# A gated linear-attention block feeding a two-layer feed-forward: units 0 to 13 interleaved step by step, and an earlier issue of the weights

## The chip, the core and the metric

The kernel runs on one core of a Trainium2 chip. The metric is the device time of one execution in microseconds (us), taken as the median of several runs. Besides these times there is one execution recorded by the hardware profiler; all starts and durations below come from it.

The core's engines work from queues of their own, each in order: PE (TensorE) multiplies matrices and writes its sums to PSUM, and its weight loads are shown as PEld; DVE (VectorE), ACT (ScalarE) and POOL (GpSimd) work on whole tiles; SP (SyncE) here only issues DMA transfers. An instruction starts when the ones before it in its queue are through and the results that it needs are there.

## The reference

```
f = 1/(1+exp(-f_logit))                        # batch 4, heads 8, 768 steps, 48 wide
for t:  state = f[t] * state + outer(k[t], v[t])      # 48 x 48 for each head
        y[t]  = q[t] @ state
x   = y, the heads side by side                # 3072 tokens x 384
h   = x @ w_in                                 # 384 -> 2048
out = max(0.01*h, h) @ w_out                   # 2048 -> 384
```

All inputs and the output are float32 in device memory. The kernel multiplies in bfloat16 and sums in float32.

## The kernel before

**Units.** The 768 steps are cut into 6 chunks of 128. One chunk of one batch is a unit, with all 8 heads; there are 24 units, chunk by chunk (units 0 to 3 are the first chunk of the four batches). Units 2x and 2x+1 are pair x. A unit goes through these steps, each a function; the letters are those that the changed kernel uses.

- **L**, `load` (L73-80): four DMAs from SP's queue, f, k, q, v in this order, 192 KB each. The tiles have 9 buffers, so nine units can be held.
- **A**, `gate_act` (L108-113): on ACT, exp and ln(1+.) turn f_logit into minus the logarithm of the gate (`lf`).
- **G**, `gate` (L115-140): on PE, a product with a triangle of ones sums `lf` along the chunk into the PSUM tile `cs`, with four narrow products for the sum at the chunk's end. ACT makes `em_t`, `a_t` and `a_end` out of it by exp. Then k is scaled by em_t (L134, on DVE for units under 13, else on POOL) and q by a_t (L135, on POOL, for unit 3 on DVE), into the two halves of the tile `kq`. For units from `TURN_DMA` = 13 on, a DMA from SP's queue then transposes `kq` into `kqT` (L138).
- **V**, `cast_v` (L142-150): two casts of v on POOL.
- **T**, `turn` (L152-162), for units under 13: PE transposes `kq`, four matmuls for the k half and four for the q half, into the PSUM tile `tp`; DVE copies each half to `kqT` after its four.
- **S**, `score` and `mask` (L164-178): eight matmuls k by q into two PSUM tiles `pw`, then two DVE multiplications by the triangle give `wm`.
- **X**, `mix` (L186-208): `wm` by v, and, from the second chunk on, the state by q, summed on PE into `py`; a DVE cast stores it as half of the pair's `xT`.
- **P**, `state` (L210-225): on PE, k by v into `pt`; two DVE additions, one POOL multiplication and two POOL casts make the state for the same batch's next chunk.
- **U** and **u**, `up2` (L233) and `up1` (L243): the first layer. `up2` gives two of the 16 hidden blocks for both units of a pair (6 matmuls of 256 columns), `up1` four blocks for one unit (12 matmuls of 128 columns). ACT applies the leaky rectifier, reading the PSUM tile `pm`, which has two buffers.
- **D**, `down` (L253-273): the second layer, 16 matmuls of 384 columns for a unit; a DVE copy to `osb` and an output DMA from SP's queue follow the last.

The PSUM tiles cs, tp, py and pt share one ring of two buffers (`ps_s`, tag "sm"): a new one waits until the one two before it has been read.

**Order.** `tc.manual_schedule()` is on: each engine runs its instructions in the order in which the functions are called. L276-445 are a list of calls written out by hand; the loop at L447-471 takes over at pair 5. In the list units 0 to 3 are carried through their attention first (L276-317), one after the other; the weights are fetched behind a small POOL copy that reads unit 3's q (L300), in eight cast DMAs issued by POOL (`load_w_in`, `load_w_out`); then the first layer of pairs 0 and 1 runs, and from L326 on the second layer of unit 0 and later units is mixed with the attention of units 4 to 12. A small DMA that reads the third part of w_out (L311) holds SP's queue until that part has come; the loads of units 4, 5, 6 stand behind it. In the loop, iteration i runs load(i+7), half of pair i//2's first layer, G and V of unit i+4, D of unit i-2, S of unit i+3, X and P of unit i+2.

Of the kernel before, what the change touches and what calls it, by code (L numbers as in the profile page):

```python
# [15 lines left out]
def kernel(  # L16
# [10 lines left out]
    nc = tc.nc  # L27

    B, H, S, D = q.shape
# [3 lines left out]
    P2 = H // 2  # L33
# [3 lines left out]

    units = [(c, b) for c in range(NCH) for b in range(B)]
    NU = len(units)
    TURN_DMA = 13  # L40
    NB = 4

    const = ctx.enter_context(tc.tile_pool(name="const", bufs=1))
# [16 lines left out]
    hold = const.tile([1, 4], FP32, tag="hold")  # L60
    WQ, OQ = FF // 4, NF // 4

    def load_w_in(i):
        nc.gpsimd.dma_start(out=w_in_b[:, :, i * WQ:(i + 1) * WQ],
                            in_=moe_w_in[:, i * WQ:(i + 1) * WQ].rearrange("(k p) f -> p k f", p=128))

    def load_w_out(i):
        nc.gpsimd.dma_start(out=w_out_b[:, i * OQ:(i + 1) * OQ, :],
                            in_=moe_w_out[i * OQ * 128:(i + 1) * OQ * 128, :].rearrange("(a p) n -> p a n", p=128))

    raw = {}
# [32 lines left out]
    st = {u: {} for u in range(NU)}  # L104
# [3 lines left out]
    def gate_act(u):  # L108
        if u >= NU:
            return  # L110
        e = work.tile([128, H, D], FP32, name="e_t", tag="e_t")
        nc.scalar.activation(e, raw[u]["f"], AF.Exp, scale=-1.0)  # L112
        nc.scalar.activation(lfs[u % 3][:, :, 0:D], e, AF.Ln, bias=1.0)  # L113

    def gate(u):  # L115
        c, b = units[u]
        lf = lfs[u % 3]
        cs = ps_s.tile([128, 512], FP32, name="cs", tag="sm")
        nc.tensor.matmul(cs[:, 0:H * D], ut, lf[:, :, 0:D], start=True, stop=True)  # L119
        if c < NCH - 1:  # L120
            for p in range(P2):
                nc.tensor.matmul(cs[:, H * D + p:H * D + p + 1], lf[:, 2 * p:2 * p + 2, :], ones_col,  # L122
                                 start=True, stop=True)
        a_t = work.tile([128, H, D], BF16, name="a_t", tag="a_t")
        em_t = work.tile([128, H, D], BF16, name="em_t", tag="em_t")
        nc.scalar.activation(em_t, cs[:, 0:H * D], AF.Exp, scale=1.0)  # L126
        nc.scalar.activation(a_t, cs[:, 0:H * D], AF.Exp, scale=-1.0)  # L127
        if c < NCH - 1:
            a_end = work.tile([128, P2], FP32, name="a_end", tag="a_end")
            nc.scalar.activation(a_end, cs[:, H * D:H * D + P2], AF.Exp, scale=-1.0)  # L130
            st[u]["a_end"] = a_end
        r = raw[u]
        kq = kqs[u % NB]
        (nc.vector if u < TURN_DMA else nc.gpsimd).tensor_mul(kq[:, 0, :, 0:D], r["k"], em_t)  # L134
        (nc.vector if u == 3 else nc.gpsimd).tensor_mul(kq[:, 1, :, 0:D], r["q"], a_t)  # L135
        if u >= TURN_DMA:
            kqT = work.tile([128, 2, P2, 128], BF16, name="kqT", tag="kqT")
            nc.sync.dma_start_transpose(out=kqT.rearrange("d a p t -> d (a p) t"),  # L138
                                        in_=kq.rearrange("t a h d -> t (a h d)"))
            st[u]["kqT"] = kqT  # L140

    def cast_v(u):  # L142
        r = raw.pop(u)
        v_b = work.tile([128, H, D], BF16, name="v_b", tag="v_b")
        nc.gpsimd.tensor_copy(out=v_b, in_=r["v"])  # L145
        v2 = v2s[u % NB]
        nc.gpsimd.tensor_copy(
            out=v2[:, :, 0:4:3, :],
            in_=r["v"].rearrange("t (p j) d -> t p (j d)", j=2)[:, :, 32:64].rearrange("t p (j e) -> t p j e", j=2))
        st[u]["v"], st[u]["v2"] = v_b, v2  # L150

    def turn(u):  # L152
        if u >= TURN_DMA:
            return
        kq = kqs[u % NB]
        tp = ps_s.tile([128, 2, P2, 128], BF16, name="tp", tag="sm")
        kqT = work.tile([128, 2, P2, 128], BF16, name="kqT", tag="kqT")
        for i in range(2):
            for p in range(P2):
                nc.tensor.transpose(tp[:, i, p, :], kq[:, i, 2 * p:2 * p + 2, :], ident)  # L160
            nc.vector.tensor_copy(out=kqT[:, i], in_=tp[:, i])  # L161
        st[u]["kqT"] = kqT

    def score(u):  # L164
        kqT = st[u]["kqT"]
        pws = [ps_w.tile([128, P2, 128], FP32, name="pw", tag="pw") for j in range(2)]
        for p in range(P2):
            for j in range(2):
                rows = slice(64 * j, 64 * j + D)
                nc.tensor.matmul(pws[j][:, p, :], kqT[rows, 0, p, :], kqT[rows, 1, p, :], start=True, stop=True)  # L170
        st[u]["pw"] = pws
        st[u]["wm"] = []

    def mask(u, js=(0, 1)):
        for j in js:
            wm = work.tile([128, P2, 128], BF16, name="wm", tag="wm", bufs=6)
            nc.vector.tensor_mul(wm, st[u]["pw"][j], ut[:, None, :].to_broadcast([128, P2, 128]))  # L177
            st[u]["wm"].append(wm)

    def pair(u):  # L180
        x = u // 2
# [91 lines left out]
            st.pop(u)  # L273


    gate_act(0)  # L276
    gate(0)
    cast_v(0)
    gate_act(1)
    turn(0)  # L280
    gate(1)
    score(0)
    mask(0)
    cast_v(1)
    gate_act(2)
    mix(0)
    state(0)
    turn(1)
    gate(2)
    score(1)  # L290
    mask(1)
    cast_v(2)
    gate_act(3)
    mix(1)
    state(1)
    turn(2)
    gate(3)
    score(2)
    mask(2)
    nc.gpsimd.tensor_copy(out=hold[:, 0:2], in_=raw[3]["q"][0:1, 0, 0:2])  # L300
    for i in range(4):
        load_w_in(i)
    cast_v(3)
    for i in range(4):
        load_w_out(i)
    mix(2)
    state(2)
    turn(3)
    score(3)
    mask(3)  # L310
    nc.sync.dma_start(out=hold[:, 2:4], in_=w_out_b[0:1, 2 * OQ, 0:4].bitcast(FP32))  # L311
    for u in (4, 5, 6):
        load(u)
    up2(0, 0)
    up2(0, 1)
    mix(3)
    state(3)
    up2(1, 0)
    up2(1, 1)
    for i in range(2, 8, 2):  # L320
        for x in range(2):
            up2(x, i)
            up2(x, i + 1)
    gate_act(4)

    down(0)  # L326
    down(1, 0, 8)
    gate(4)
    cast_v(4)
    gate_act(5)  # L330
    load(7)
    down(1, 8)
    down(2, 0, 8)
    turn(4)
    score(4)
    mask(4)
    down(2, 8)
    gate(5)
    cast_v(5)
    gate_act(6)  # L340
    load(8)
    down(3, 0, 8)
    mix(4)
    state(4)
    turn(5)
    down(3, 8)
    up1(4, 0)
    up1(4, 1)
    score(5)
    mask(5)  # L350
    up1(4, 2)
    gate(6)
    cast_v(6)
    load(9)
    up1(4, 3)
    mix(5)
    state(5)
    gate_act(7)
    down(4, 0, 8)
    turn(6)  # L360
    down(4, 8)
    up1(5, 0)
    score(6)
    mask(6)
    up1(5, 1)
    gate(7)
    cast_v(7)
    load(10)
    up1(5, 2)
    mix(6)  # L370
    state(6)
    up1(5, 3)
    gate_act(8)
    down(5, 0, 6)
    turn(7)
    down(5, 6, 8)
    score(7)
    mask(7)
    down(5, 8, 12)
    mix(7)  # L380
    state(7)
    load(11)
    load(12)

    def attend(u):
        gate(u)
        cast_v(u)
        gate_act(u + 1)

    up2(3, 0)  # L390
    attend(8)
    up2(3, 1)
    up2(3, 2)
    down(5, 12)
    load(13)
    turn(8)
    up2(3, 3)
    score(8)
    mask(8)
    attend(9)  # L400
    up2(3, 4)
    mix(8)
    state(8)
    load(14)
    up2(3, 5)
    up2(3, 6)
    turn(9)
    up2(3, 7)
    score(9)
    mask(9)  # L410
    down(6, 0, 6)
    attend(10)
    mix(9)
    state(9)
    load(15)

    up2(4, 0)
    up2(4, 1)
    attend(11)
    down(6, 6)  # L420
    turn(10)
    up2(4, 2)
    score(10)
    mask(10)
    up2(4, 3)
    turn(11)
    mix(10)
    state(10)
    score(11)
    mask(11)  # L430
    load(16)

    up2(4, 4)
    attend(12)
    up2(4, 5)
    down(7, 0, 8)
    attend(13)
    mix(11)
    turn(12)
    up2(4, 6)  # L440
    state(11)
    up2(4, 7)
    score(12)
    mask(12)
    down(7, 8)

    for i in range(10, NU + 2):  # L447
        x, h = divmod(i, 2)
        if i + 7 < NU:
            load(i + 7)  # L450
        if i < NU:
            up2(x, 4 * h)
            up2(x, 4 * h + 1)
        if i + 4 < NU:
            gate(i + 4)
            cast_v(i + 4)
        down(i - 2, 0, 8)
        if i < NU:
            up2(x, 4 * h + 2)
        gate_act(i + 5)  # L460
        if i + 3 < NU:
            score(i + 3)
            mask(i + 3, (0,))
        if i + 2 < NU:
            mix(i + 2)
            state(i + 2)
        if i + 3 < NU:
            mask(i + 3, (1,))
        if i < NU:
            up2(x, 4 * h + 3)  # L470
        down(i - 2, 8)
# [30 lines left out]
```

## Time and profile before

| | |
|---|---|
| median of 3 runs | 205.68 us (205.6 to 206.25) |
| the profiled execution | 205.76 us, of which its span, first to last instruction, is 204.0 us |
| busy: PE, DVE, ACT, POOL | 176.1, 90.4, 101.6, 81.9 us |
| start to first layer, 0 to 27.0 us | PE busy 12.67 of 27.00 us |
| first layer of pairs 0 and 1, 27.0 to 41.5 us | PE busy 14.08 of 14.50 us |
| L326 to the loop, 41.5 to 107.1 us | PE busy 56.39 of 65.60 us |
| the loop, 107.1 to 204.0 us | PE busy 92.99 of 96.90 us |
| granted PE clock | 1.00 throughout |

The stages are cut at starts that the timeline gives: the first matmul of L239 at 27.00, of L259 at 41.50, and the loop's first L239 at 107.10 us. In lines of the timeline the columns are start, duration, engine, line, operation, output<-input, how many; in square brackets stands how long the engine was idle before, and what it waited for. The end of a matmul is modelled and lies after the start of the next, so the cost of a group is read from its start to the start of the next group.

### The profile page before, as it was taken

How to read it: one execution, taken by the hardware profiler on the slowest of the kernel's cores; microseconds unless marked ns; L12 is line 12 of the kernel's file. 1: busy time of each engine (PE TensorE's matmuls, PEld its weight loads, DVE VectorE, ACT ScalarE, POOL GpSimd, SP SyncE). 2: the span in 40 equal slices, each digit the busy share in tenths (PEclk: the TensorE clock that was granted, in tenths of full speed). 3: DMA queues.
4: the chain of work that ended last, by engine and by line, in shares of the span. 5: the costliest groups of instructions: out<-in, count | busy, mean ns of one | idle time of the engine just before them, and what ended most of it. 6: DMA issues, size and time to landing. Idle time of an engine off the chain costs nothing.

```text
span 204.0 us, 5211 instructions
## 1 busy us (share of the span) xinstructions
PE 176.1 (86%) x2112; PEld 127.0 (62%) x2112; DVE 90.4 (44%) x183; ACT 101.6 (50%) x214; POOL 81.9 (40%) x172
## 2 busy tenths in 40 slices
PE   0465489997798888887979999999999999999992
PEld 0344357765486756665757777777767777677760
DVE  5367731014655656656663355335543344321120
ACT  4532125843343718674656565756576563444400
POOL 8356952003405514653574457454755434000000
PEclk9999999999999999999999999999999999999999
DMA  6992799999899999996326999999996332111112
GB/s 129 216 216 59 102 184 202 171 203 201 189 259 198 198 193 203 188 221 134 72 55 148 147 221 199 201 171 195 195 204 89 90 93 51 42 39 42 39 39 79
DMA packets 118796, 29.96 MB, mean 147 GB/s; under 512 B 111988, under 2 KB 118772, under 8 KB 118772
## 3 DMA queue, kind: packets, MB, share of 16 engines
q1 hardware_dynamic: 114916, 26.39, 64.8%
q0 software_dynamic: 3712, 3.15, 10.2%
q8 instruction: 16, 0.26, 0.5%
q10 hardware_dynamic: 144, 0.10, 0.1%
q14 instruction: 8, 0.07, 0.1%
HBM read 25.17 MB, written 4.72 MB: 147 GB/s over the span
## 4 chain that ended last, share of the span: by engine, by line
PE 76%; DVE 9%; ACT 6%; issue 3%; DMA 2%; SPq 1%; POOL 1%
PE pm L259 29%; PE pm L239 29%; PE py L206 4%; PE tp L160 4%; PE pw L170 4%; DVE kqT L161 3%; DVE wm L177 3%; ACT em_t L126 2%; PE pm L249 2%; PE cs L119 2%; DMA f_raw<-in_f_logit_dram 2%; PE pt L218 2%; DVE xT L208 2%; SPq L78 1%; ACT a_t L127 1%
## 5 line engine op out<-in xcount | busy, mean ns | idle before, releaser
L241 ACT ACTIVATE gT<-pm 128x512 bf16<-128x512 f32 x88 | 52.3, 597 | 63.1 <-PE pm L239 61.7
L239 PE MATMUL pm<-xT,w_in_b 128*128 128x256 bf16 x528 | 69.3, 276 | 1.3 <-DVE xT L208 0.9
L259 PE MATMUL pm<-w_out_b,gT 128*128 128x384 bf16 x384 | 69.5, 326 | 0.0
L239 PEld LDWEIGHTS <-w_in_b 128*128 128x128 bf16 x528 | 50.6, 99 | 12.8 <-issue 2.7
L177 DVE TENSOR_TENSOR wm<-pw,ut 128x512 bf16<-128x512 f32 x48 | 31.9, 688 | 40.9 <-PE pw L170 40.6
L259 PEld LDWEIGHTS <-gT 128*128 128x128 bf16 x384 | 36.3, 98 | 20.5
L135 POOL TENSOR_TENSOR kq<-q_raw,a_t 128x384 bf16<-128x384 f32 x23 | 21.4, 930 | 39.8 <-ACT a_end L130 24.6
L265 DVE COPY osb<-pm 128x384 f32<-128x384 f32 x23 | 12.8, 558 | 33.0 <-PE pm L259 32.7
L160 PE MATMUL tp<-ident,kq 128*128 128x128 bf16 x104 | 11.6, 244 | 10.4 <-DVE kqT L161 7.6
L222 POOL TENSOR_TENSOR sf<-sf,a_end 128x192 f32<-128x192 f32 x20 | 10.2, 509 | 23.6 <-DVE sf L221 23.6
L126 ACT ACTIVATE em_t<-cs 128x384 bf16<-128x384 f32 x24 | 11.7, 487 | 15.5 <-PE cs L122 15.4
L134 POOL TENSOR_TENSOR kq<-k_raw,em_t 128x384 bf16<-128x384 f32 x11 | 10.0, 913 | 22.5 <-issue 18.3
L208 DVE CAST xT<-py 128x384 bf16<-128x384 f32 x24 | 13.3, 553 | 9.8 <-PE py L206 9.7
L160 PEld LDWEIGHTS <-kq 128*128 128x128 bf16 x104 | 8.6, 109 | 13.5 <-issue 10.7
L161 DVE COPY kqT<-tp 128x512 bf16<-128x512 bf16 x26 | 11.0, 424 | 11.8 <-PE tp L160 11.7
L225 POOL CAST sb<-sf 64x192 bf16<-64x192 f32 x40 | 13.7, 342 | 2.5
L112 ACT ACTIVATE e_t<-f_raw 128x384 f32<-128x384 f32 x24 | 12.6, 527 | 3.8 <-DMA f_raw<-in_f_logit_dram 3.8
L206 PE MATMUL py<-wm,v_b 128*32 128x128 bf16 x192 | 9.4, 231 | 4.8 <-DVE wm L177 4.8
L119 PE MATMUL cs<-lf,ut 128*128 128x384 bf16 x24 | 8.5, 356 | 5.3 <-ACT lf L113 5.3
L113 ACT ACTIVATE lf<-e_t 128x384 bf16<-128x384 f32 x24 | 12.6, 524 | 0.8
L145 POOL CAST v_b<-v_raw 128x384 bf16<-128x384 f32 x24 | 12.1, 505 | 0.0
L134 DVE TENSOR_TENSOR kq<-k_raw,em_t 128x384 bf16<-128x384 f32 x13 | 7.4, 573 | 10.5 <-ACT em_t L126 10.5
(41 smaller groups left out, 143.4 us busy)
## 6 DMA issues: line engine op xcount, KB each, us to landing
f_raw<-in_f_logit_dram SPq DMA_DIRECT2D x24, 192.0 KB, 3.3
k_raw<-in_k_dram SPq DMA_DIRECT2D x24, 192.0 KB, 3.7
q_raw<-in_q_dram SPq DMA_DIRECT2D x24, 192.0 KB, 3.7
v_raw<-in_v_dram SPq DMA_DIRECT2D x24, 192.0 KB, 3.9
out_dram<-osb SPq DMA_DIRECT2D x23, 192.0 KB, 2.0
w_in_b<-in_moe_w_in_dram POOLq DMA_DIRECT2D x4, 384.0 KB, 7.3
w_out_b<-in_moe_w_out_dram POOLq DMA_DIRECT2D x4, 384.0 KB, 11.3
kqT<-kq SPq DMA_TRANSPOSE x11, 3.9
```

The lines of the kernel that those rows point to most:

```text
L126: nc.scalar.activation(em_t, cs[:, 0:H * D], AF.Exp, scale=1.0)
L134: (nc.vector if u < TURN_DMA else nc.gpsimd).tensor_mul(kq[:, 0, :, 0:D], r["k"], em_t)
L135: (nc.vector if u == 3 else nc.gpsimd).tensor_mul(kq[:, 1, :, 0:D], r["q"], a_t)
L160: nc.tensor.transpose(tp[:, i, p, :], kq[:, i, 2 * p:2 * p + 2, :], ident)
L161: nc.vector.tensor_copy(out=kqT[:, i], in_=tp[:, i])
L177: nc.vector.tensor_mul(wm, st[u]["pw"][j], ut[:, None, :].to_broadcast([128, P2, 128]))
L206: nc.tensor.matmul(py[32 * r:32 * r + 32, kk, :], lhsT, rhs, start=not begun[r], stop=left[r] == 0)
L208: nc.vector.tensor_copy(out=pair(u)["xT"][:, :, u % 2, :], in_=py)
L225: nc.gpsimd.tensor_copy(out=state_b[b][rows, :, j * D:j * D + D], in_=sf[rows])
L239: nc.tensor.matmul(pm[:, a], w_in_b[:, kk, ff * 128:(ff + 1) * 128], s["xT"][:, kk], start=(kk == 0), stop=(kk == NK - 1))
L241: nc.scalar.activation(s["g"][:, 2 * i:2 * i + 2], pm, AF.Prelu, alpha=0.01)
L259: nc.tensor.matmul(s["pm2"], g[:, ff, u % 2], w_out_b[:, ff, :], start=(ff == 0), stop=(ff == NF - 1))
```

## The change

- Copies of a unit's turned k and q: all eight transposes are issued, then the two copies (T).
- The scaling of k becomes a step of its own, **K**: on DVE for units 0 to 7, on POOL for units from 8 on, there still inside `gate`. q is always scaled on POOL, unit 3's too.
- `TURN_DMA` is 14: unit 13 is turned by PE, in the loop's first iteration.
- The POOL copy that holds back the weights reads unit 3's k. The first two parts of w_in are issued ahead of unit 3's G (so of its scaling of q), the other two and w_out behind its V.
- The list of calls is replaced by strings of steps with another order. P of units 0 to 3 goes into the first layer. Four units' loads, L4 to L7, now stand together ahead of the first layer (before: L4 to L6); L8 to L16 follow singly, L16 as the list's last step, behind D7.

```
-    TURN_DMA = 13
+    TURN_DMA = 14
...
-        (nc.vector if u < TURN_DMA else nc.gpsimd).tensor_mul(kq[:, 0, :, 0:D], r["k"], em_t)
-        (nc.vector if u == 3 else nc.gpsimd).tensor_mul(kq[:, 1, :, 0:D], r["q"], a_t)
+        if u >= 8:
+            scale_k(u)
+        nc.gpsimd.tensor_mul(kq[:, 1, :, 0:D], raw[u]["q"], a_t)
...
+    def scale_k(u):
+        (nc.vector if u < 8 else nc.gpsimd).tensor_mul(kqs[u % NB][:, 0, :, 0:D], raw[u]["k"], st[u].pop("em"))
...
                 nc.tensor.transpose(tp[:, i, p, :], kq[:, i, 2 * p:2 * p + 2, :], ident)
+        for i in range(2):
             nc.vector.tensor_copy(out=kqT[:, i], in_=tp[:, i])
...
+    def do(line):
+        for word in line.split():
+            op, arg = word[0], word[1:]
...
+    do("A0 G0 K0 V0 A1 T0 S0 G1 K1 V1 X0 A2 T1 G2 S1 K2 V2 X1 A3 T2")
+    nc.gpsimd.tensor_copy(out=hold[:, 0:2], in_=raw[3]["k"][0:1, 0, 0:2])
+    do("I0 I1 G3 S2 K3 V3 I2 I3 O0 O1 O2 O3 X2 T3 S3")
     nc.sync.dma_start(out=hold[:, 2:4], in_=w_out_b[0:1, 2 * OQ, 0:4].bitcast(FP32))
+    do("L4 L5 L6 L7 U0.0 U0.1 X3 U0.2 U0.3 P0 U1.0 U1.1 P1 U1.2 U1.3 P2 U0.4 U0.5 P3")
+    do("U1.4 U1.5 U0.6 U0.7 U1.6 U1.7 A4")
+    do("D0:0-16 D1:0-12 G4 K4 V4 D1:12-16 D2:0-8 T4 D2:8-12 A5 S4 G5 K5 V5 D2:12-16 L8 D3:0-8 X4 P4 D3:8-16 L9 T5")
+    do("u4.0 S5 u4.1 A6 u4.2 X5 P5 L10 G6 K6 V6 u4.3 D4:0-8 T6 D4:8-12 A7 S6 D4:12-16 L11")
+    do("u5.0 u5.1 X6 G7 K7 V7 P6 u5.2 L12 u5.3 T7 A8 D5:0-8 S7 G8 V8 D5:8-16 X7 P7 L13")
+    do("U3.0 U3.1 U3.2 T8 A9 U3.3 G9 V9 S8 U3.4 U3.5 X8 T9 A10 U3.6 P8 L14 G10 V10 S9 U3.7 D6:0-8 X9 P9 T10")
+    do("A11 D6:8-16 L15 U4.0 G11 V11 S10 U4.1 U4.2 X10 P10 T11 A12 U4.3 G12 V12 S11 U4.4 D7:0-8 X11 P11 T12")
+    do("A13 U4.5 G13 V13 S12 U4.6 U4.7 A14 D7:8-16 L16")
...
         down(i - 2, 0, 8)
+        if i + 3 < NU:
+            turn(i + 3)
```

Letters and numbers: `U3.4` is up2 of pair 3, step 4; `u4.0` is up1 of unit 4, step 0; `D2:8-12` is down of unit 2, blocks 8 to 11; `I0`, `O0` are the first parts of w_in and w_out. All that the list from L276 to L445 held is dropped.

More of the change, by code (lines that the diff above doesn't have):

```diff
@@ L131, in gate @@
             st[u]["a_end"] = a_end
-        r = raw[u]
+        st[u]["em"] = em_t
         kq = kqs[u % NB]
-        (nc.vector if u < TURN_DMA else nc.gpsimd).tensor_mul(kq[:, 0, :, 0:D], r["k"], em_t)
-        (nc.vector if u == 3 else nc.gpsimd).tensor_mul(kq[:, 1, :, 0:D], r["q"], a_t)
+        if u >= 8:
+            scale_k(u)
+        nc.gpsimd.tensor_mul(kq[:, 1, :, 0:D], raw[u]["q"], a_t)
         if u >= TURN_DMA:
@@ L178, in mask, with score_mask @@
             st[u]["wm"].append(wm)
+    def score_mask(u):
+        score(u)
+        mask(u)
     def pair(u):
@@ L273, in down @@
             st.pop(u)
[L276 to L310, printed above, removed]
-    nc.sync.dma_start(out=hold[:, 2:4], in_=w_out_b[0:1, 2 * OQ, 0:4].bitcast(FP32))
[L312 to L445, printed above, removed]
+    def do(line):
+        for word in line.split():
+            op, arg = word[0], word[1:]
+            if op == "D":
+                u, span = arg.split(":")
+                lo, hi = span.split("-")
+                down(int(u), int(lo), int(hi))
+            elif op in "Uu":
+                x, i = arg.split(".")
+                (up2 if op == "U" else up1)(int(x), int(i))
+            else:
+                {"A": gate_act, "G": gate, "K": scale_k, "V": cast_v, "T": turn, "S": score_mask,
+                 "X": mix, "P": state, "L": load, "I": load_w_in, "O": load_w_out}[op](int(arg))
```

## The prediction

> **What bounds the kernel now.** I read the slices first, then PE's busy time by stage, then what PE waited for, then the timeline around the longest waits, last SP's queue.
>
> ```profile
> PE   0465489997798888887979999999999999999992
> PEclk9999999999999999999999999999999999999999
> DMA  6992799999899999996326999999996332111112
> ```
>
> PE is full from slice 21 on (about 107 us, the loop) and has holes before. The stage view has the amounts, PE busy in the third column:
>
> ```profile
> 0.00:27.00 27.00, 12.67 (x144) 8.82 (x145) 16.23 (x35) 9.11 (x21) 18.48 (x47) 1.00 0.80 145
> 41.50:107.10 65.60, 56.39 (x772) 40.55 (x770) 36.83 (x76) 33.42 (x78) 26.57 (x55) 1.00 0.87 179
> ```
>
> So 14.3 us stand open before the first layer and 9.2 us between D0 and the loop. Only there can a new order gain; the loop's 96.9 us stay. PE's waits from 41.5 to 107.1 us (total, times, longest):
>
> ```profile
> PE tp L160 <- DVE kqT L161: 5.5, 9, 0.8
> PE pw L170 <- DVE kqT L161: 0.7, 2, 0.5
> PE pm L239 <- DVE xT L208: 0.7, 2, 0.4
> ```
>
> One in every unit: the q half's transposes stand still until the k half has been copied out of the same PSUM tile. On PE's timeline (unit 6):
>
> ```profile
> 62.82 0.39 PE L160 MATMUL tp<-ident,kq 128*128 128x128 bf16 x4
> 63.72 0.38 PE L160 MATMUL tp<-ident,kq 128*128 128x128 bf16 x4 [0.52 <-DVE kqT L161]
> 63.94 0.49 PE L259 MATMUL pm<-w_out_b,gT 128*128 128x384 bf16 x2
> ```
>
> T takes 1.12 us of PE here; four transposes with nothing in between take 0.22 (63.72 to 63.94), so eight 0.44.
>
> **Part 1, start to first layer (27.0 us to 23.2).** I put the new order on the durations of this stretch: em starts 0.60 after cs, 0.53 later a DVE scaling of 0.56 can start, POOL's of q 0.91; four cold transposes take 0.58, a copy 0.42, S 0.61, two masks 1.28, cast 0.56. T0's q half follows q's scaling at 7.22, its copies end at 8.67, S0 starts at 8.72. G1 now stands behind S0: cs1 at 9.3, em1 at 9.95 (before 9.10), but nothing of P0 is left in the way. T1 starts at 11.3 (12.51), T2 at 16.0 (18.04), T3 at 20.6 (24.26): some 4.7 us a unit for 5.5, paced by S, masks, K, T. Eight transposes 1.15, two copies 0.84, S3 0.6: the first layer at 23.2. f_raw isn't late: A2 is the last that waits for it.
>
> The weights' copy stood behind P1's POOL work and ran at 20.09. Now only V2 (over at about 15.9) and k's arrival are ahead: landing takes 3.7 us, unit 3's k is issued at 11.98. So I0, I1 go out from 16 to 17.6 (0.78 each), q3 follows at 18.75 to 19.7, V3 to 20.5, the six others by 25 (27.15 before). Moved to POOL, q3 costs 0.91 for DVE's 0.64 but ends before k3 is scaled (20.6). The moved P0 to P2 take 3 x 0.34 of PE in the first layer; pairs of up2 there run at 1.50 us against 1.31 in the loop (held by the two pm buffers), which hides most. I add 0.4 and drop as much (PE's 0.46 and 0.24 waits at 30 us). D0 starts at 23.2 + 14.4 = **37.6** (41.5). w_out's last part would land near 36, D0 needs it at 39.5; L4's f near 39, G4 needs it at 42: covered by 3 us each. DMA is full in this stretch, so if the early issue gained nothing, L4 would be late by about 0.5.
>
> **Part 2, D0 to the loop (65.6 us to 59.4).** Work that can't go, each from start to next start: 24 groups of first layer at 0.66 = 15.8; 16 half D at 1.31 = 21.0; 10 G at 0.27, 9 T at 0.44, 9 S at 0.33, 8 X at 0.55, 8 P at 0.17 = 15.5. Sum 52.3. The old stage has 13.3 above it: 9.2 of waits, the rest tails around them. Walking the new list with the same latencies, these waits come back:
>
> - S behind T's two copies: T's start to S is now 0.64 + 0.84 + 0.06 = 1.54, of which T itself is 0.44 and the step in between 0.66 to 0.9. S4, S5, S6, S11, S12 wait 0.3 to 0.6: 2.2 in all. DVE's other work (osb, xT, P's additions) stands ahead of the copies.
> - T behind the scaled q: for units 8 on POOL scales k, then q: em's start to q's end is 2.35 us (101.78 to 104.13, unit 13), for 1.92 with k on DVE (45.84 to 47.76). T7, T9, T10, T11 wait 1.5 in all; T10 also because P8's 1.25 of POOL precedes K10.
> - the "sm" ring of two: P6 behind xT6, G10 behind T9's copies, T12 behind xT11: 1.0.
> - G behind A on ACT: cs6 0.3, cs9 0.6; U3.0 behind xT7: 0.45. Sum 1.3.
>
> 6.0, and some 1.1 of tails: 52.3 + 7.1 = 59.4. The loop starts at 37.6 + 59.4 = **97.0** (107.1), 10.1 earlier.
>
> The scaling moved to POOL appears in no row beside this order. Bounds: the loop's row, 0.91 a unit, and the worst of POOL's q rows, 1.23; five units then cost PE between 0 and 5 x 0.32 = 1.6. I take 0.91, the median of all rows. [...]
>
> **Part 3, the loop (96.9 us to 99.8).** T13 now on PE: 0.44, and S13 behind its copies 0.45 (1.54 less T13 and one group of 0.66). Then SP's queue, in order:
>
> ```profile
> 107.89 0.36 SPq L266 DMA_DIRECT2D out_dram<-osb  x1
> 108.34 0.39 SPq L78 DMA_DIRECT2D f_raw<-in_f_logit_dram  x1
> 108.78 0.69 SPq L78 DMA_DIRECT2D k_raw<-in_k_dram  x1
> 109.52 0.57 SPq L78 DMA_DIRECT2D q_raw<-in_q_dram  x1
> 110.14 1.16 SPq L78 DMA_DIRECT2D v_raw<-in_v_dram  x1
> 111.54 2.42 SPq L138 DMA_TRANSPOSE kqT<-kq  x1
> ```
>
> The loop starts at 107.10; unit 14's transpose is issued 4.44 later behind out7 and L17, lands by 5.6 after that, and S14 follows at 117.3, with no slack. In the changed list L16 stands behind out7 too: four more issues, 3.2 us at these rows and 4.0 at the 0.99 that eight issues in a row took from 82.1 to 90.0. The transpose goes out 7.6 to 8.4 after the loop's start and lands 4.2 to 5.6 later, at 11.8 to 14.0; S14 stands at 10.2 + 0.9 = 11.1. PE waits **0.7 to 2.9; I take 2.0**, since a deeper backlog is nearer to the long landing. Later transposes recover: SP's iteration (0.45 + 3.2 + about 2) is shorter than PE's 6.59. Loop: 96.9 + 0.9 + 2.0 = 99.8.
>
> **Sum.** 97.0 + 99.8 = 196.8 of span; the profiled execution has 1.76 around its span (205.76 and 204.0): 198.6. The median, 205.68, is within 0.1 of the profiled one.
>
> **The rivals.**
> 1. *Denser than I think*: the waits in part 2 are taken from a hand-made order, and errors of a few tenths can hide each other; at half (−3.5) and with the transpose at its lower bound (−1.3): 193.8. For it: the loop has all these steps and no waits. Against: the loop leaves two full iterations between steps.
> 2. *The latency chain holds the middle*: what T loses returns before S and behind POOL. If only half of part 2's 6.2 comes: 201.7. For it: DVE's copies stay, POOL gets more; against: other matmuls now stand between T and S.
> 3. *SP becomes the bound, slower than before*: the list delays L16, and from then on out (0.97), four loads and a transpose (2.42) must pass SP in 6.59 us. At 0.99 a load this is 7.35, at 1.1 it is 7.8. Seven iterations still load, each costing PE the excess: 198.6 + 7 x 0.76 = 203.9, or 207.1. It decides from 7.7 on. For it: single issues of 1.2 to 1.9 us while DMA is full; against: in the loop's rows loads take 0.7 to 0.8 on average and DMA has room.
> 4. *The change doesn't do it*: the copies' wait is not between halves but the PSUM ring's, and the earlier weights wait for DMA anyway: 205.
>
> **How the numbers follow.** Forecast, 196.5 to 200.5: 0.56. Rival 1: 0.17. Rival 2: 0.16. Rival 3: 0.08, most of it above 206.3. Rival 4: 0.03. The range leaves out rival 3's upper part, rival 4 and the lowest part of rival 1: 193.8 to 203.0. About 0.3% is what a measurement of this kernel tells from no change; faster 0.89, same 0.03, slower 0.08.
>
> **What would show it.** Part 1: first L239 at about 23, the first w_in issue at 16, first L259 at 37 to 38. Part 2: no "tp <- kqT" wait, T's eight matmuls in one row, the loop's first L239 at 96 to 98; instead waits of pw for kqT and of tp for POOL's kq. Part 3: S14 waiting for the DMA kqT, and SP's unit-14 transpose behind eight loads. The forecast fails if S14's wait recurs in every iteration, if PE waits for f_raw or for weights, or if G waits for ACT more than twice.

## The result and the profile after

The changed kernel takes 196.69 us (196.53 to 196.99) beside 205.97 for the kernel before: a ratio of 0.955 (95% interval 0.953 to 0.958), 9.3 us less. Its profiled execution took 196.84 us with a span of 195.1.

The same slices as before, PE and DMA:

```profile
PE   0566899999979989999999799999999999999992
DMA  6998999999999999972099999999894134011112
```

PE is fuller up to the loop, and DMA's gap in slice 4, where it waited for the weights to be issued, is gone (8 tenths busy, for 2). A new hole stands in PE's slice 23 (107 to 112 us), and DMA is nearly idle in slices 19 and 20, before the loop. (Slices are counted from 1 here; the prediction's "slice 21" counts from 0.) The stages, cut at the same events (first layer, D0, the loop's first group of the first layer); PE busy is the third column:

```profile
0.00:22.42 22.42, 11.19 (x132) 7.59 (x133) 13.27 (x28) 9.22 (x21) 15.82 (x40) 1.00 0.95 177
36.55:96.11 59.56, 55.30 (x772) 40.09 (x770) 33.61 (x71) 33.59 (x78) 30.72 (x59) 1.00 0.89 184
96.11:195.10 98.99, 93.60 (x1092) 67.59 (x1089) 35.50 (x69) 50.67 (x102) 34.76 (x66) 1.00 0.62 126
```

The first layer starts 4.6 us earlier (22.42 for 27.00), D0 to the loop is 6.0 shorter (59.56 for 65.60), the loop 2.1 longer (98.99 for 96.90). PE's waits between D0 and the loop (total, times, longest; the first four of seven rows, 4.1 us in all):

```profile
PE tp L164 <- DVE xT L217: 1.2, 3, 0.4
PE tp L164 <- POOL kq L136: 0.7, 1, 0.7
PE pw L175 <- DVE kqT L166: 0.6, 3, 0.2
PE cs L119 <- ACT lf L113: 0.5, 1, 0.5
```

The wait of tp for kqT, 5.5 us before, is gone. T is now one row of eight matmuls, 0.45 long from its start to the next group's (unit 4):

```profile
43.31 0.61 PE L164 MATMUL tp<-ident,kq 128*128 128x128 bf16 x8
43.76 0.81 PE L268 MATMUL pm<-w_out_b,gT 128*128 128x384 bf16 x4
```

What the loop lost is on SP's timeline and, for S14, on PE's:

```profile
96.89 0.36 SPq L275 DMA_DIRECT2D out_dram<-osb  x1
97.34 0.39 SPq L78 DMA_DIRECT2D f_raw<-in_f_logit_dram  x1
...
102.02 1.93 SPq L78 DMA_DIRECT2D q_raw<-in_q_dram  x1
104.05 0.76 SPq L78 DMA_DIRECT2D v_raw<-in_v_dram  x1
104.91 1.44 SPq L139 DMA_TRANSPOSE kqT<-kq  x1
```

```profile
106.28 0.82 PE L248 MATMUL pm<-xT,w_in_b 128*128 128x256 bf16 x6
108.58 0.40 PE L175 MATMUL pw<-kqT 48*128 48x128 bf16 x8 [1.48 <-DMA kqT<-kq]
```

Unit 14's transpose goes out 8.8 us after the loop's start, behind eight transfers (those of L16 and L17), where before it was 4.4; PE stands still for 1.48 us.

### The profile page after: what moved, and what is told of

Read it like the earlier page. It is cut to its first block, busy times and chain, and to the rows that moved or that the text cites. A ratio compares the mean times of both kernels' runs of the same rounds, so it can differ in the third digit from the quotient of the medians.

```text
span 195.1 us, 5235 instructions
## 1 busy us (share of the span) xinstructions
PE 174.2 (89%) x2120; PEld 126.5 (65%) x2120; DVE 87.0 (45%) x179; ACT 102.3 (52%) x214; POOL 88.3 (45%) x178
## 4 chain that ended last, share of the span: by engine, by line
PE 82%; DVE 6%; DMA 3%; ACT 3%; issue 2%; POOL 2%; POOLq 0%
PE pm L248 30%; PE pm L268 30%; PE py L215 5%; PE pw L175 5%; PE tp L164 4%; DVE kqT L166 3%; PE cs L119 2%; PE pm L258 2%; PE pt L227 2%; DMA kqT<-kq 2%; DVE xT L217 2%; POOL kq L136 2%; DMA f_raw<-in_f_logit_dram 1%; DVE wm L182 1%; ACT em_t L126 1%
## 5 line engine op out<-in xcount | busy, mean ns | idle before, releaser
L136 POOL TENSOR_TENSOR kq<-q_raw,a_t 128x384 bf16<-128x384 f32 x24 | 22.4, 935 | 21.2 <-ACT a_end L130 21.1
L144 POOL TENSOR_TENSOR kq<-k_raw,em_t 128x384 bf16<-128x384 f32 x16 | 14.6, 914 | 28.5 <-issue 19.7
L175 PE MATMUL pw<-kqT 48*128 48x128 bf16 x192 | 10.4, 232 | 4.8 <-DVE kqT L166 3.4
L164 PE MATMUL tp<-ident,kq 128*128 128x128 bf16 x112 | 10.9, 245 | 3.6 <-DVE kq L144 1.2
L175 PEld LDWEIGHTS <-kqT 48*128 48x128 bf16 x192 | 6.6, 99 | 8.7 <-issue 3.4
L164 PEld LDWEIGHTS <-kq 128*128 128x128 bf16 x112 | 8.1, 108 | 6.2 <-DVE kq L144 2.2
```

Source lines behind the costliest of these rows:

```text
L136: nc.gpsimd.tensor_mul(kq[:, 1, :, 0:D], raw[u]["q"], a_t)
L144: (nc.vector if u < 8 else nc.gpsimd).tensor_mul(kqs[u % NB][:, 0, :, 0:D], raw[u]["k"], st[u].pop("em"))
```

## The experiments

For each kernel the stages of its profiled execution, in us; the events that cut them are the same:

| kernel | start to first layer | to D0 | D0 to the loop | loop | span | ratio to before (95%) |
|---|---|---|---|---|---|---|
| before | 27.00 | 14.50 | 65.60 | 96.90 | 204.0 | |
| changed | 22.42 | 14.13 | 59.56 | 98.99 | 195.1 | 0.955 (0.953 to 0.958) |
| e1, T alone | 25.86 | 14.19 | 60.67 | 96.88 | 197.6 | 0.970 (0.967 to 0.973) |
| e2, all but T | 23.82 | 14.35 | 64.08 | 100.35 | 202.6 | 0.989 (0.985 to 0.993) |
| e3, weights late | 25.04 | 14.46 | 59.56 | 99.34 | 198.4 | 0.975 (0.972 to 0.977) |
| e4, L16 early | 22.44 | 14.72 | 59.56 | 97.48 | 194.2 | 0.952 (0.950 to 0.954) |
| e5, K on DVE | 22.51 | 14.46 | 60.65 | 99.38 | 197.0 | 0.969 (0.966 to 0.972) |
| e6, old middle | 22.77 | 13.86 | 60.66 | 96.61 | 193.9 | 0.952 (0.950 to 0.954) |
| e7, fewer waits | 22.49 | 13.20 | 54.78 | 97.33 | 187.8 | 0.926 (0.924 to 0.929) |
| e8, K behind masks | 22.70 | 13.64 | 59.93 | 99.43 | 195.7 | 0.961 (0.959 to 0.964) |
| e9, changed again | 22.52 | 13.55 | 59.74 | 99.99 | 195.8 | 0.959 (0.956 to 0.962) |

The profiled execution of e2 is the longest of its four (204.37 us, median 203.28), that of e7 the shortest of its six (189.62, median 190.71). The measurements were made on several chips, each beside the kernel before, so differences of a few tenths between medians of different rows say little; the ratios and the stages say more.

**e1, the transposes' edit alone** (in the kernel before):

```
                 nc.tensor.transpose(tp[:, i, p, :], kq[:, i, 2 * p:2 * p + 2, :], ident)
+        for i in range(2):
             nc.vector.tensor_copy(out=kqT[:, i], in_=tp[:, i])
```

> The kernel before with one edit: all eight transposes of a unit, then its two copies (the order of the list and the weights as before). Theory H (the halves' wait is most of what the middle lost, and goes by itself): no wait of tp for kqT; PE saves 0.52 to 0.68 in units 5 to 12, where a step stands between T and S, gives back 0.1 to 0.2 before S in some, and saves 0.27 in units 0 to 4, where the chain through T is what counts: 4 to 5.5 us less, 200.5 to 202. Rival O (the new order carries the gain; with the old order the wait only moves in front of S): 1.5 us less at the most, 204.3 or more.

Measured 199.62 us: 5.9 us less than the kernel before beside it (205.49) by an edit of one line, more than theory H said (4 to 5.5). D0 to the loop fell from 65.60 to 60.67, the start by 1.14. In the waits of that stage no row of tp for kqT is left, and those of pw for kqT rose only from 0.7 to 1.8:

```profile
PE pw L171 <- DVE kqT L162: 1.8, 4, 0.8
```

Rival O falls.

**e2, everything but that edit** (the changed kernel with the line above taken out again):

> The changed kernel with one edit undone: each half's copy follows its four transposes again. Theory H: each of 14 units turned on PE loses the 0.52 wait again, less what S waited (0.2): 5 to 6.5 us more than the changed kernel, 201.5 to 203. Rival O: the new order hides the halves' wait too, 2 us more at the most, below 199.

Measured 203.28 us, 0.3 above theory H's range (201.5 to 203). D0 to the loop is 64.08: the old T costs 4.5 us here, though the list leaves a step between T and S nearly everywhere. Over the whole execution the wait within T is back:

```profile
PE tp L164 <- DVE kqT L165: 7.7, 13, 0.8
```

The new order doesn't hide a wait that stands within one step. The ratios multiply, nearly: 0.970 x 0.989 = 0.959, measured together 0.955.

**e3, the weights no earlier than before:**

```
-    nc.gpsimd.tensor_copy(out=hold[:, 0:2], in_=raw[3]["k"][0:1, 0, 0:2])
-    do("I0 I1 G3 S2 K3 V3 I2 I3 O0 O1 O2 O3 X2 T3 S3")
+    do("G3 S2 K3")
+    nc.gpsimd.tensor_copy(out=hold[:, 0:2], in_=raw[3]["q"][0:1, 0, 0:2])
+    do("V3 I0 I1 I2 I3 O0 O1 O2 O3 X2 T3 S3")
```

> The changed kernel, but the weights' holding copy reads unit 3's q and stands behind unit 3's scaling of q, and all eight weight DMAs behind it and V3, as far as possible as before. Theory W (the shorter chain of units 0 to 3 and the earlier issue need each other): the first w_in part goes out at about 20 and lands 5 to 6.5 later, the first layer starts at 25.2 to 26.6 for 22.4, and the whole is 2.8 to 4.2 us longer: 199.5 to 201. Rival C (the head start comes from the chain of units 0 to 3 alone): 0.5 more at the most.

Measured 200.28 us, as theory W says. The first part of w_in goes out at 19.83 for 15.86, and the first layer has a wait that no other kernel shows at this size:

```profile
25.04 2.74 PE L248 MATMUL pm<-xT,w_in_b 128*128 128x256 bf16 x12 [2.19 <-DMA w_in_b<-in_moe_w_in_dram]
```

The 2.6 us here (25.04 less 22.42) stay to the end. The shorter chain alone gives 0.8 of the 3.4 us between e1's start (25.86) and 22.42; with the early issue it gives all of it. That the early issue alone would bring nothing is argued, from e1's first layer, which waits for no weights; no run has it alone.

**e4, L16 ahead:**

```
-    do("A11 D6:8-16 L15 U4.0 ...
+    do("A11 D6:8-16 L15 L16 U4.0 ...
...
-    ... U4.6 U4.7 A14 D7:8-16 L16")
+    ... U4.6 U4.7 A14 D7:8-16")
```

> The changed kernel with L16 right behind L15 instead of behind D7's output. Theory Q (unit 14's DMA transpose is late only because eight loads stand ahead of it on SP's queue): the transpose goes out 4.4 to 5 after the loop's start for 8.8, S14's wait of 1.48 falls to 0.3 or less, 1.2 to 1.5 us less than the changed kernel: 195.2 to 195.5. Rival B (DMA is behind as a whole at this point, whatever SP's order): the wait stays above 1.0.

Measured 195.79 us; the loop took 97.48 for 98.99. The transpose goes out 4.4 after the loop's start (96.72):

```profile
99.79 0.96 SPq L78 DMA_DIRECT2D v_raw<-in_v_dram  x1
101.10 1.36 SPq L139 DMA_TRANSPOSE kqT<-kq  x1
```

S14 no longer waits for it. Theory Q holds: it was SP's order, not DMA's load. The other runs agree: in every kernel with L16 at the list's end (changed, e2, e3, e5, e8, e9) S14 waits 1.1 to 1.7 us for the transpose, in e4, e6 and e7, where L16 goes out earlier, not at all. The median, 195.79, is 0.9 below the changed kernel's first one where 1.2 to 1.5 was expected; in the profiled execution the first layer took 0.6 longer (14.72), and how that varies from kernel to kernel stands at the end.

**e5, k scaled on DVE up to unit 13:**

```
-        (nc.vector if u < 8 else nc.gpsimd).tensor_mul(kqs[u % NB][:, 0, :, 0:D], raw[u]["k"], st[u].pop("em"))
+        (nc.vector if u < 14 else nc.gpsimd).tensor_mul(kqs[u % NB][:, 0, :, 0:D], raw[u]["k"], st[u].pop("em"))
```

> The changed kernel with k scaled on DVE up to unit 13 (as the kernel before had it up to unit 12), where the changed one uses POOL from unit 8 on. Theory R (in units 8 to 13 T waits for the PSUM ring, that is for xT on DVE, and not for POOL): nothing gained, within 0.4 us of the changed kernel's 196.7; DVE's 0.56 ahead of xT and the copies can even cost 0.2 or 0.3. Rival K (the move to POOL costs PE what POOL is slower by): 0.6 to 1.6 us less, 195.1 to 196.1.

Measured 198.78 us. Both theories are wrong: with this order the slower engine is the better one, by 1.1 us between D0 and the loop. The waits of T for xT are as in the changed kernel; X has got longer. X10 on PE's timeline of e5 (a part):

```profile
86.23 0.35 PE L215 MATMUL py<-kqT,sb 128*32 128x128 bf16 x12
...
87.17 0.24 PE L215 MATMUL py<-wm,v_b 128*32 128x128 bf16 x4 [0.30 <-DVE wm L182]
87.22 0.24 PE L215 MATMUL py<-wm,v 128*32 128x128 bf16 x4
87.39 0.34 PE L227 MATMUL pt<-v_b,kq 128*128 128x96 bf16 x4
```

From X's start to P's it is 1.16 us, in the changed kernel 0.51:

```profile
85.38 0.35 PE L215 MATMUL py<-kqT,sb 128*32 128x128 bf16 x12
85.89 0.34 PE L227 MATMUL pt<-v_b,kq 128*128 128x96 bf16 x4
86.62 0.61 PE L164 MATMUL tp<-ident,kq 128*128 128x128 bf16 x8 [0.39 <-DVE xT L217]
```

DVE's timeline of e5 has the reason, the row of K11 and the masks of unit 10 behind it:

```profile
85.36 0.56 DVE L144 TENSOR_TENSOR kq<-k_raw,em_t 128x384 bf16<-128x384 f32 x1 [1.11 <-ACT em_t L126]
85.83 1.28 DVE L182 TENSOR_TENSOR wm<-pw,ut 128x512 bf16<-128x512 f32 x2
```

G11 is called ahead of S10, so K11 stands ahead of S10's masks in DVE's queue, and there it waits for em; the masks could have started at about 84.9, 0.4 after S10 (84.48), as in the changed kernel (83.64 and 84.07).

**e6, the new start with the old middle.** From D0 to the loop the list of before, k scaled on DVE up to unit 12, `TURN_DMA` = 13; the eight transposes together:

```
-    TURN_DMA = 14
+    TURN_DMA = 13
...
-    do("D0:0-16 D1:0-12 G4 K4 V4 D1:12-16 D2:0-8 T4 ...
+    down(0)
+    down(1, 0, 8)
+    gate(4)
+    scale_k(4)
...
```

> The changed kernel up to A4 (units 0 to 3, the weights, the first layer), with the eight transposes together, but from D0 to the loop the list, the scaling and the limit 13 of the kernel before. Theory F (the stages add up): D0 at 36.5 to 37.2, then the 60.7 us that the list of before took with the new T, then a loop of 96.9 without T13 and without the late transpose: a span of 194.1 to 194.8, 195.8 to 196.6 in all: no slower than the changed kernel, its new middle being worth 1.1 before the loop and costing 2.1 in it. Rival J (the old middle was cut to the later start, and with L4 to L16 no earlier than before it waits for its loads): 198 or more, with PE or ACT waits for f_raw.

Measured 195.66 us, 0.1 below theory F's range (195.8 to 196.6), with its 60.7 between D0 and the loop (60.66). The new middle list, with its POOL scaling, is worth 1.1 us (59.56), the very amount that e5 loses with k on DVE, and loses more in the loop (98.99 for 96.61), by L16's place and T13. Both kernels gain from T and from the start.

**e7, the places where PE still waits.** e4 with the middle list changed throughout in this manner (the strings joined, two stretches of them):

```
-X5 P5 L10 G6 K6 V6 u4.3 D4:0-8 T6 D4:8-12 A7 S6 D4:12-16 L11 u5.0 u5.1 X6 G7 K7 V7 P6 u5.2 L12 u5.3
+X5 P5 L10 u4.3 G6 K6 V6 A7 D4:0-14 T6 D4:14-16 L11 u5.0 S6 u5.1 G7 K7 V7 u5.2 X6 L12 u5.3 P6
...
-X10 P10 T11 A12 U4.3 G12 V12 S11 U4.4 D7:0-8 X11 P11 T12 A13 U4.5 G13 V13 S12 U4.6
+A12 X10 P10 U4.3 T11 G12 V12 U4.4 S11 D7:0-8 A13 X11 P11 U4.5 T12 G13 V13 U4.6 S12
```

> The changed kernel with L16 behind L15 and with the middle's list changed at each place where its trace shows PE waiting: a piece of D or U is put between X and the step that waits for the ring (T10, T11, T12, P6, G6) or for xT7 (U3.0), between T and S (S4, S5, S6), between G6 and T6, and A9 goes ahead of the first layer's group. Theory M (each of these waits is real time on PE and its cover is free): of 4.1 us of waits in this stage about 0.6 stay; with the 1.2 of the earlier L16 the whole takes 192 to 193.5. Rival N (the waits come back elsewhere, ACT or DVE being the next bound): 194.8 or more.

Measured 190.71 us (189.62 to 191.59), 7.4% faster than the kernel before (0.924 to 0.929). All that PE waits for from D0 (35.69) to 110 us:

```profile
PE tp L164 <- POOL kq L136: 0.5, 1, 0.5
PE pw L175 <- DVE kqT L166: 0.2, 1, 0.2
```

Theory M holds in kind and gives too little (192 to 193.5). In this stage the waits fell by 3.6 us (4.1 to 0.5), the stage by 4.8 (59.56 to 54.78); most of the rest came off what the profile calls busy (PE 55.30 to 54.21 us). That fits a tail at each wait, time in which PE does nothing new but is still shown as busy: in the changed kernel's rows under e5, P10's four matmuls take 0.17 of PE, so T10 starts 0.56 after them (86.06 to 86.62), and only 0.39 of this is called a wait. In the profiled execution the first layer was shorter too (13.20 for 14.13).

**e8, K on DVE but behind the masks**, and **e9, the changed kernel again** beside it. e8 is e5 with K a step of its own up to unit 13, in the list behind S; unit 9's place stands for those of units 9 to 13:

```
-G9 V9 S8 U3.4
+G9 S8 K9 V9 U3.4
```

> The changed kernel with k scaled on DVE up to unit 13, as in the run with K on DVE (198.78), but in units 9 to 13 behind the masks of the unit before in DVE's queue, where that run had it ahead of them. Theory D (K on DVE cost time because it stood in front of the masks and waited there for em, so that X came late): X takes 0.5 again, and the whole is within 0.5 us of the changed kernel. Rival E (DVE has no room for 0.56 more in a unit, wherever it stands): 198 or more, and xT or the copies late instead.

> The changed kernel unedited, on the same chip as the run beside it: 196.7 within 0.6 us by either theory; it is the measure for the other.

Measured 197.76 and 197.62 us: the same. e9 is 0.9 above the first measurement of this kernel, 0.3 outside what was expected of it, so e8 is judged by its stages: X10 takes 0.51 again (85.32 to 85.83), D0 to the loop 59.93, for 60.65 in e5 and 59.56 and 59.74 in the changed kernel. Theory D holds: K's place in DVE's queue was the cost. A small rest stays: T11 waits 0.6 for xT (0.39 in the changed kernel). xT10 starts there right behind K11 (86.18), and K11 takes 1.05 us in e8 (85.21 to 86.26), for 0.56 in e5. It starts while POOL still scales q (84.94 to 85.85), and V's first cast, which POOL starts at 85.79, takes 0.83 for 0.50; each is longer where the other engine was still at work. In e5 K11 was nearly through when q's scaling started (85.84). That the overlap is the cause is argued from these rows; no run was made for it.

## Why the prediction was right, step by step

The sum gave a span of 196.8 us for a measured 195.1: part 1 was 1.05 too long and part 3 0.8, part 2 0.2 too short. The forecast, 198.6, was 1.9 too long: the median, 196.69, lies only 0.2 inside the lower end of the range (196.5); the same kernel measured again gave 197.62.

- *Part 1* was right in kind, 0.8 us too long at the first layer and 1.05 at D0. Predicted: weights at 16, first layer at 23.2, D0 at 37.6. Measured: 15.86, 22.42, 36.55. Of the transposes that it calls cold the traces show only that they are longer: in the changed kernel the row of T3's eight is 1.03 us (at 20.00), that of T4's 0.61 (at 43.31), with the clock granted at 1.00 in both stages; no run shows why. Two copies took 0.76 for 0.84, and from T1 to T3 a T came every 4.3 to 4.65 us for 4.6 to 4.7. A3 waited for f_raw too (1.02 us of ACT), against the prediction's "A2 is the last"; PE did not feel it, since G3 followed T2 without a wait. e1 and e3 split the 4.6: T gave 1.1, the new order with the early weights 3.4, and the order without the weights 0.8 (25.04 against e1's 25.86).
- *Part 2*, 59.4 for a measured 59.56, was right by terms that made up for each other. The waits predicted at 6.0 are 4.1 in the trace; the tails, taken at 1.1, are 3.0 (PE's 55.30 busy less 52.3 of work; the small steps of that sum come to 15.4 and not 15.5). The most wrong term is S behind T's copies, 0.6 for 2.2: S11 and S12 did not wait, and S4, S5 and S6 waited 0.2 instead of 0.3 to 0.6, or 0.36 with their tails (S4: 1.46 from T4's start, less 0.45 of T and 0.65 of the step between). U3.0 and G9 came within 0.1 of their size. P6, T12 and G10 were put at 1.0 together: P6 waited 0.32, T12 0.39, G10 not at all; G6, put down to ACT at 0.3, waited 0.40 for the ring's xT. T10 and T11, put down to POOL, waited for the ring's xT as well, 0.39 each, and T7 and T9 did not wait. T6's 0.70 was missed: P5's POOL work (54.66 to 56.18) stands ahead of unit 6's scaling of q, the very thing that I had looked for at T10.
- *The scaling on POOL* was the step with the wrong sign. I bounded it by 0 below and 1.6 above and took no cost; beside K on DVE ahead of the masks (e5) it is a gain of about 1 us, beside K on DVE behind them (e8) of 0.2 to 0.4. I had asked what 0.91 for 0.56 does to T, and not what the 0.56 stands in front of on DVE. With K on DVE as in e5 the span was 1.2 to 1.9 us longer than in the changed kernel's two executions (197.0; 195.8 and 195.1), though the scaling itself is shorter there (0.56 for 0.91); with K on DVE behind the masks, as in e8, it was 195.7, between the two.
- *Part 3* had the mechanism, shown by e4. The loop took 98.99 for 99.8. S14 waited 1.48 for 2.0: the transpose went out later than my bounds (8.8 for 7.6 to 8.4) and landed sooner, 3.6 after its issue for 4.2 to 5.6. T13 with S13 cost 0.45 + 0.19 for 0.9. But "later transposes recover" holds only in part: in e9, the same kernel, S17 waits 0.87 us too (2.4 with S14's), and in e2 1.25.
- *The rivals.* The first (denser) and the second (latency holds the middle) fell for the change, since the stage came out at its forecast; that a denser middle is to be had, e7 shows. The third fell in its size: in the changed kernel's execution no S after S14 waits for a transpose, but in e9 and e2 one more does, S17, so SP has less room than the sum took. The fourth fell with e1: the order within T alone takes the halves' wait away.

What I did not separate beforehand is the two edits of part 2. The stage's length was right; that nearly all of it would come from one line, and that the rewritten list would be paid back in the loop, only e1, e2 and e6 showed.

## What to carry to other kernels

When an engine waits in the same way in every unit, look inside the step first: here a write to the second half of a PSUM tile stood behind the read of the first (5.5 us of PE's waits from D0 to the loop), and taking the copies together was by itself worth 6 of 9.3 us, where all the rest of the change by itself was worth 2. When work is moved between engines, its duration can matter less than what stands behind it in the queue that it leaves, and whether it waits there for something late: here 0.91 us of POOL for 0.56 of DVE made the stage from D0 to the loop 1.1 us shorter (59.56 for e5's 60.65). And a step that is moved takes its DMA issues along: L16 at the list's end made a transpose late and cost PE 1.5 us in the loop, where the change had moved nothing but T13.

## What was not expected of the hardware

The first layer of pairs 0 and 1 took 13.2 to 14.7 us in kernels whose code up to D0 is the same. ACT's timeline shows when the pace changes; first e4, then e7 (rows of the rectifier, one execution for each step of `up2`):

```profile
25.22 0.60 ACT L250 ACTIVATE gT<-pm 128x512 bf16<-128x512 f32 x1 [0.68 <-PE pm L248]
27.16 0.60 ACT L250 ACTIVATE gT<-pm 128x512 bf16<-128x512 f32 x1 [1.34 <-PE pm L248]
28.35 0.60 ACT L250 ACTIVATE gT<-pm 128x512 bf16<-128x512 f32 x1 [0.59 <-PE pm L248]
29.18 1.27 ACT L250 ACTIVATE gT<-pm 128x512 bf16<-128x512 f32 x2 [0.23 <-PE pm L248]
```

```profile
25.13 0.60 ACT L250 ACTIVATE gT<-pm 128x512 bf16<-128x512 f32 x1 [0.55 <-PE pm L248]
26.23 1.25 ACT L250 ACTIVATE gT<-pm 128x512 bf16<-128x512 f32 x2 [0.50 <-PE pm L248]
27.73 1.25 ACT L250 ACTIVATE gT<-pm 128x512 bf16<-128x512 f32 x2 [0.25 <-PE pm L248]
```

A group of six matmuls takes 1.28 us at first (23.94 to 25.22 in e4) and then 0.75; the change comes after 28 us in e4 and at 25 in e7. PE is dense from 22 us on in both (2.00 us busy of the 2.00 from 22 to 24), and the profile grants the clock at 1.00 throughout; what makes the pace change is not shown. Whether it explains the spread of e7's times (189.62 to 191.59) is not shown either, since only the shortest of them has a profile. It does not explain e9's 0.9 above the first measurement: in its profiled execution e9's first layer was the shorter one (13.55 for 14.13) and its loop the longer (99.99 for 98.99).
